# More units by rows, w_mod earlier, and group loads moved to other slots in a fused attention and gMLP kernel

## The chip, the cores and the metric

One core of one Trainium2 chip. The metric is the time of one execution in device microseconds (us).

## The reference, cut to what matters

```python
mod = (silu(c) @ w_mod).reshape(1, 6, 1, 512)         # sa, ca, ga, sb, cb, gb
h = layernorm(x) * (1 + ca) + sa
q = (h @ wq)                                           # 32 heads of 128; 8 groups of 4 heads share k, v
p = softmax(q @ k.T / sqrt(128))                       # 2048 queries x 2048 keys
x = x + ga * ((p @ v) @ wo)
h = layernorm(x) * (1 + cb) + sb
z = gelu(h @ w_in); z1, z2 = halves of z; z2 = layernorm(z2)
x = x + gb * ((z1 * (w_sp @ z2 + b_sp)) @ w_out)
```

## The kernel before

A *unit* is one query tile of 128 rows of one group of 4 heads: 8 groups x 16 tiles = 128 units. *Iteration* u is the stretch of code with the scores of unit u, in eight *slots*: in each, two score matmuls, one exp of 1024 columns on ScalarE (ACT), a part of an older unit's weighted sum, and one matmul of the q projection or the output projection. A plain unit computes its scores transposed, and its weighted sum uses p as the weights, 64 matmuls of 129 columns. A unit *by rows* computes scores row-wise, divides by the row sum on VectorE (DVE), turns each head with a DMA transpose issued from SyncE, and needs 16 matmuls of 512 columns, but two iterations later.

```python
TURN_A, TURN_B = 3 * CT, (HKV - 1) * NT                # 12, 112
def by_rows(u):
    return TURN_A <= u < TURN_B and u % 2 == 0
def pv_at(u):                                          # iteration of the weighted sum
    return u + 3 if by_rows(u) else u + 1
...
def turn_rows(u, hh):                                  # two slots after the head's second exp
    ... row sum, reciprocal, multiply on DVE ...
    nc.sync.dma_start_transpose(out=pTs[u][:, :, hh * P : (hh + 1) * P], in_=pn[hh])
...
def mod_rows():                                        # gate rows through DRAM
    ...
        nc.gpsimd.dma_start(out=line[:]..., in_=modc[:, cols])
        nc.gpsimd.dma_start(out=rows[:], in_=line[:].partition_broadcast(P))
...
at(9, 4, mod_cols_b)                                   # at(iteration, slot, work)
at(10, 4, mod_rows)
...
for g in range(1, HKV):
    it = (g - 1) * NT
    at(it + 7, 6, lambda g=g: load_k(g))               # SyncE, a transposing load
    at(it + 8, 3, lambda g=g: load_v(g))               # POOL
    at(it + 9, 3, lambda g=g: load_wo(g, nc.gpsimd))   # POOL
    at(it + 7, 3, lambda g=g: load_wq(g, nc.gpsimd))   # POOL
```

`pn[0..2]` lie in the memory of `win_sb`, `pn[3]` in that of `wmod_a`; a unit's head can be exponentiated into them only when the turn of two units before has been read out.

Of the kernel before, what the change touches and what calls it, by code (L numbers as in the profile page):

```python
# [10 lines left out]
BF16 = mybir.dt.bfloat16  # L11
# [4 lines left out]
P = 128  # L16
# [559 lines left out]
def kernel(  # L576
# [19 lines left out]
    nc = tc.nc  # L596
    _, S, D = A_x.shape
    _, HKV, SK, DH = A_k_cache.shape
# [6 lines left out]
    NT = S // P  # L605
    NDT = D // P
    NKT = SK // P
    NFT = FH // P
    NCH = S // 512
    CT = 512 // P  # L610
    FC = _f_chunk(FH)
    NFHC = FH // FC
    NSLOT = NKT // 2
# [14 lines left out]
    win_dram = B_w_in.rearrange("(dt p) f -> p dt f", p=P)  # L628
# [15 lines left out]
    late = free_b.enter_context(tc.tile_pool(name="late", bufs=2, side="right"))  # L644
# [12 lines left out]
    win_sb = win_t[:].rearrange("p (k f) -> p k f", k=NDT)  # L657
# [13 lines left out]
    def bank2():  # L671
        return psum.tile([P, 1024], FP32, name="s_ps")
# [45 lines left out]
    def load_wq(g, engine):  # L718
        wqs[g] = early.tile([P, NDT, REP * DH], BF16, name="wq_g")
        engine.dma_start(  # L720
            out=wqs[g][:], in_=wq_dram[:, :, g * REP * DH : (g + 1) * REP * DH]
        )

    def load_v(g):
        v1 = late.tile([P, NKT, DV], BF16, name="v1")
        nc.gpsimd.memset(v1[:, :, DH:DV], 1.0)
        if g > 0:
            nc.gpsimd.dma_start(out=v1[:, :, 0:DH], in_=v_dram[:, g])
        else:
            nc.sync.dma_start(out=v1[:, 0 : NKT // 2, 0:DH], in_=v_rows)  # L730
            nc.sync.dma_start(
                out=v1[:, NKT // 2 : NKT, 0:DH], in_=v_dram[:, 0, NKT // 2 : NKT]
            )
        groups[g]["v1"] = v1

    def load_wo(g, engine):
        wo_g = late.tile([P, REP, D], BF16, name="wo_g")
        engine.dma_start(out=wo_g[:], in_=wo_dram[:, g * REP : (g + 1) * REP, :])
        groups[g]["wo"] = wo_g

    def load_k(g):
        kT = early.tile([P, SK], BF16, name="kT")
        nc.sync.dma_start_transpose(out=kT[:], in_=A_k_cache[0, g])
        groups[g] = dict(kT=kT)
# [154 lines left out]
    for k in range(2):  # L899
        for dt in (2 * k, 2 * k + 1):  # L900
# [3 lines left out]
            else:  # L904
                nc.scalar.activation(
                    out=dst,
                    in_=src,
# [17 lines left out]
    for hf, copy in enumerate((nc.vector.tensor_copy, nc.scalar.copy)):  # L925
        copy(
            out=qTs[0][:, 2 * hf : 2 * hf + 2, 0:P],
            in_=q_ps[hf][:, 0 : 2 * P].rearrange("p (h q) -> p h q", h=2),
# [33 lines left out]
    NU = HKV * NT  # L962


    TURN_A, TURN_B = 3 * CT, (HKV - 1) * NT

    def by_rows(u):
        return TURN_A <= u < TURN_B and u % 2 == 0

    def pv_at(u):  # L970
        return u + 3 if by_rows(u) else u + 1

    rsums, pTs, onorms, oTs, xaccs, o_pss, h2Ts = {}, {}, {}, {}, {}, {}, {}
    later = {}

    def at(it, slot, fn):
        later.setdefault((it, slot), []).append(fn)

    def qk(u, i):
        g, j = divmod(u, NT)  # L980
        b, jj = g * NCH + j // CT, j % CT
        if i == 0:
            if TURN_A <= u <= TURN_B + 1 and u % 2 == 1:
                pTs[u] = wspp.tile([P, NT, 512], BF16, name="wsp")
            else:
                pTs[u] = late.tile([P, NKT, 512], BF16, name="pT")
            if by_rows(u):
                rsums[u] = stat.tile([P, NSLOT], FP32, name="rs")
        s_ps = bank2()
        if by_rows(u):  # L990
            hh, half = divmod(i, 2)
            for c in range(2):
                k0 = (2 * half + c) * 512
                nc.tensor.matmul(  # L994
                    s_ps[:, c * 512 : (c + 1) * 512],
                    lhsT=qTs[b][:, hh, jj * P : (jj + 1) * P],
                    rhs=groups[g]["kT"][:, k0 : k0 + 512],
                    start=True,
                    stop=True,
                )  # L1000
            nc.scalar.activation(  # L1001
                out=pn[hh][:, half * HK : (half + 1) * HK],
                in_=s_ps[:],
                func=ACT.Exp,
                scale=inv_sqrt_dh,
                accum_out=rsums[u][:, i : i + 1],
            )
            if half == 1:
                at(*divmod(u * NSLOT + i + 2, NSLOT), lambda: turn_rows(u, hh))
            return  # L1010
        for h in range(2):
            kt = 2 * i + h
            nc.tensor.matmul(  # L1013
                s_ps[:, h * 512 : (h + 1) * 512].rearrange("p (r q) -> p r q", r=REP),
                lhsT=groups[g]["kT"][:, kt * P : (kt + 1) * P],
                rhs=qTs[b][:, :, jj * P : (jj + 1) * P],
                start=True,
                stop=True,
            )
        nc.scalar.activation(  # L1020
            out=pTs[u][:, 2 * i : 2 * i + 2, :],
            in_=s_ps[:].rearrange("p (k q) -> p k q", k=2),
            func=ACT.Exp,
            scale=inv_sqrt_dh,
        )
# [150 lines left out]
    def load_wsp(tile_, t, st):  # L1176
        nc.sync.dma_start_transpose(
            out=tile_[:, st, :],
            in_=B_w_sp[t * 512 : (t + 1) * 512, st * P : (st + 1) * P],
        )  # L1180

    wsp = [None] * NCH
# [33 lines left out]
    ln1_at(2, (2, 4), (3, 1), (4, 5))  # L1216
    ln1_at(3, (5, 1), (5, 5), (7, 4))
    at(2, 5, lambda: nc.gpsimd.dma_start(out=wmod_b, in_=wmod_dram[:, :, 2 * D : NMOD]))
    at(TURN_B + 3, 5, lambda: nc.gpsimd.dma_start(out=win_sb, in_=win_dram))
    at(9, 4, mod_cols_b)  # L1220
    at(10, 4, mod_rows)

    def set_fill(b):


        hole = TURN_A + 1 if (TURN_A + 1) // CT == b - 1 else None
        fs = qproj(b, list(range(REP)), 0, 512, ("misc", "o_ps" if hole else "misc"))
        for k, fn in enumerate(fs):
            it, slot = (b - 1) * CT + k // NDT, k % NDT
            if hole:  # L1230
                it, slot = hole, k // 2
            if b == 1:
                it, slot = 2 + (10 + k) // 16, (5 + k // 2) % 8
            elif b == 2:
                it, slot = (5, k // 2) if k < 8 else (it, slot)
            fill.setdefault((it, slot), []).append(fn)
# [1 line left out]
    def wsp0():  # L1238
        wsp[0] = wspp.tile([P, NT, 512], BF16, name="wsp")

    at(TURN_B + 4, 0, wsp0)
    for st in range(NT):
        at(TURN_B + 4 + st // 2, 2 + 4 * (st % 2), lambda st=st: load_wsp(wsp[0], 0, st))
    for g in range(1, HKV):
        it = (g - 1) * NT
        at(it + 7, 6, lambda g=g: load_k(g))
        at(it + 8, 3, lambda g=g: load_v(g))
        at(it + 9, 3, lambda g=g: load_wo(g, nc.gpsimd))
        at(it + 7, 3, lambda g=g: load_wq(g, nc.gpsimd))


    zs = {}
# [90 lines left out]
    for it in range(NU + 6):  # L1343
        if it < NU:
            if it % CT == 0 and it // CT + 1 < NB:
                set_fill(it // CT + 1)
        elif it == NU:
            free_a.close()
            z2p = fast.enter_context(tc.tile_pool(name="z2p", bufs=1))
            zs["z2"] = z2p.tile([P, NT, FH], BF16, name="z2")  # L1350
        pvs = [u for u in (it - 3, it - 1) if 0 <= u < NU and pv_at(u) == it]
        wos = [u for u in (it - 5, it - 3) if 0 <= u < NU and pv_at(u) + 2 == it]
        wf = [fn for u in wos for fn in wo_proj(u)]
        for i in range(NSLOT):
            for fn in later.pop((it, i), []):
                fn()
            if it < NU:
                qk(it, i)
            if len(pvs) == 1:
                pv_part(pvs[0], i, NSLOT)  # L1360
            elif pvs:
                n = NSLOT // 2
                pv_part(pvs[i // n], i % n, n)
            for fn in fill.pop((it, i), []):
                fn()
            if i >= NSLOT - len(wf):
                wf[i - NSLOT + len(wf)]()
            if it >= NU:
                zrun(3)
        for u in wos:  # L1370
            if u >= (HKV - 1) * NT:
                ln2(it, u % NT)
        if it == NU + 2:
            free_b.close()
            mlp = fast.enter_context(tc.tile_pool(name="mlp", bufs=1, side="right"))
            zs["z1T"] = mlp.tile([P, NFT, S], BF16, name="z1T")
            wout_sb = mlp.tile([P, NFT, D], BF16, name="wout_sb")
            bsp_bc = mlp.tile([P, S], BF16, name="bsp_bc")
            nc.gpsimd.dma_start(out=wout_sb[:], in_=wout_dram)
            nc.gpsimd.dma_start(out=bsp_bc[:], in_=B_b_sp.partition_broadcast(P))  # L1380
# [11 lines left out]
    for f in range(NFT):  # L1392
# [6 lines left out]
        out=ok1[:], in0=rall[:], scalar1=1.0 / SAFE, scalar2=None, op0=ALU.is_ge  # L1399
# [8 lines left out]
        out=bad[:], in0=okm[:], scalar1=-1.0, scalar2=1.0, op0=ALU.mult, op1=ALU.add  # L1408
# [137 lines left out]
```

## Time and profile before

| | before |
|---|---|
| median of the first 3 executions | 1316.68 us (1314.65 to 1318.89) |
| span of the profiled execution | 1314.1 us |
| TensorE busy | 99% |
| ACT, DVE busy | 84%, 50% |
| turns (512 KB SBUF to SBUF), issue to landing | 4.2 / 4.6 / 13.3 us least, median, most |

Busy shares are averages, and TensorE's 99% hide short waits. How start times show them, and the lines, are in the prediction.

### The profile page before, as it was taken

To read this page: it belongs to the slowest core of one execution; us is meant where nothing else is said; L and a number is where in the kernel's file an instruction comes from. 1 tells how busy PE (TensorE), PEld (TensorE's weight loads), DVE (VectorE), ACT (ScalarE), POOL (GpSimd) and SP (SyncE) were. 2 spreads that over 40 slices of the span, in tenths; PEclk is the share of its full clock that TensorE was granted. 3 is DMA by queue.
4 is the path that set the end of the run, shared out by engine and by line. 5 is a ranking of instruction groups with operands and counts; after the bars stand their busy time and mean duration, and the time that the engine had idled before them with its cause. 6 is when DMAs were issued, how large, how long until landed. Compare 5 with 4: busy or idle time off the path is not lost.

```text
span 1314.1 us, 25092 instructions
## 1 busy us (share of the span) xinstructions
PE 1305.1 (99%) x9959; PEld 755.5 (57%) x9959; DVE 657.4 (50%) x1612; ACT 1105.0 (84%) x1461; POOL 52.0 (4%) x96
## 2 busy tenths in 40 slices
PE   9999999999999999999999999999999999999998
PEld 5666555555555555555555555555556666644445
DVE  6624445444454544444455544444452566784444
ACT  7899999999999999999999999999998899650000
POOL 1101000000000000000000000000000000120000
PEclk9999999999999999999999999999999999999999
DMA  7554988878988888988897877688762232143200
GB/s 181 123 67 58 180 161 141 140 125 158 153 144 138 144 141 138 135 142 157 153 143 129 155 141 144 124 166 151 140 126 76 45 62 48 29 117 80 69 21 27
DMA packets 537741, 156.79 MB, mean 119 GB/s; under 512 B 527280, under 2 KB 533680, under 8 KB 537616
## 3 DMA queue, kind: packets, MB, share of 16 engines
q1 hardware_dynamic: 530592, 135.97, 60.3%
q0 software_dynamic: 4432, 16.91, 4.6%
q10 hardware_dynamic: 2592, 2.23, 0.5%
q8 instruction: 80, 1.31, 0.4%
q14 instruction: 45, 0.37, 0.1%
HBM read 21.89 MB, written 2.10 MB: 18 GB/s over the span
## 4 chain that ended last, share of the span: by engine, by line
PE 98%; DMA 1%; DVE 0%; issue 0%; ACT 0%; ACTq 0%; DVEq 0%
PE o_ps L1069 21%; PE s_ps L1013 20%; PE o_ps L1048 13%; PE s_ps L994 13%; PE misc L1101 8%; PE misc L944 8%; PE misc L1426 7%; PE s_ps L1260 2%; PE s_ps L1299 2%; PE o_ps L1447 1%; DMA pT<-wmod_a 1%; PE o_ps L785 1%; PE s_ps L1447 1%; PE misc L854 0%; PE o_ps L944 0%; DVE hT L813 0%
## 5 line engine op out<-in xcount | busy, mean ns | idle before, releaser
L1020 ACT ACTIVATE wsp<-s_ps 128x1024 bf16<-128x1024 f32 x408 | 416.2, 1025 | 19.5 <-PE s_ps L1013 3.5
L1013 PE MATMUL s_ps<-qT,kT 128*128 128x512 bf16 x1248 | 370.9, 379 | 1.9 <-ACT wmod_a L1001 1.6
L1001 ACT ACTIVATE win_sb<-s_ps 128x1024 bf16<-128x1024 f32 x300 | 307.0, 1025 | 6.2 <-ACT win_sb L1001 0.8
L1069 PEld LDWEIGHTS <-wsp 128*128 128x128 bf16 x3264 | 218.5, 98 | 96.3
L1069 PE MATMUL o_ps<-v,wsp 128*128 128x129 bf16 x3264 | 251.6, 220 | 0.0
L994 PE MATMUL s_ps<-kT,qT 128*128 128x512 bf16 x800 | 237.9, 379 | 0.0
L1048 PE MATMUL o_ps<-pT,v 128*128 128x512 bf16 x800 | 237.3, 379 | 0.0
L1020 ACT ACTIVATE pT<-s_ps 128x1024 bf16<-128x1024 f32 x216 | 217.3, 1026 | 20.6 <-PE s_ps L1013 8.3
L1101 PE MATMUL misc<-wo_g,oT 128*128 128x512 bf16 x512 | 194.0, 379 | 0.0
L1013 PEld LDWEIGHTS <-kT 128*128 128x128 bf16 x1248 | 121.0, 98 | 117.0 <-issue 4.4
L944 PE MATMUL misc<-hT,wq_g 128*128 128x512 bf16 (+2 forms) x520 | 187.0, 371 | 0.1
L1069 PEld LDWEIGHTS <-pT 128*128 128x128 bf16 x1728 | 115.3, 98 | 49.6
L955 DVE CAST qT<-misc 128x512 bf16<-128x512 f32 x125 | 85.5, 684 | 112.2 <-PE misc L944 112.2
L1048 PEld LDWEIGHTS <-v 128*128 128x128 bf16 x800 | 78.2, 98 | 94.4
L1069 PE MATMUL o_ps<-v,pT 128*128 128x129 bf16 x1728 | 132.5, 220 | 0.0
L1057 DVE CAST oT<-o_ps 128x512 bf16<-128x512 f32 x50 | 34.6, 691 | 173.7 <-PE o_ps L1048 173.7
L1035 DVE TENSOR_SCALAR win_sb<-win_sb,rall 128x2048 bf16<-128x2048 bf16 x150 | 113.0, 753 | 5.7 <-DVE rall L1034 0.5
L994 PEld LDWEIGHTS <-qT 128*128 128x128 bf16 x800 | 78.2, 98 | 52.5 <-issue 0.2
L1001 ACT ACTIVATE wmod_a<-s_ps 128x1024 bf16<-128x1024 f32 x100 | 102.4, 1024 | 2.3 <-DMA pT<-wmod_a 2.3
L1426 PE MATMUL misc<-wsp,z 128*128 128x512 bf16 (+2 forms) x560 | 100.7, 336 | 0.0
L1080 DVE RECIPROCAL rall<-o_ps 128x2 f32<-128x2 f32 x156 | 26.6, 170 | 135.1 <-PE o_ps L1069 131.4
L1031 DVE TENSOR_TENSOR tot<-rs 128x1 f32<-128x1 f32 x200 | 30.7, 154 | 120.6 <-ACT win_sb L1001 119.1
(106 smaller groups left out, 856.5 us busy)
## 6 DMA issues: line engine op xcount, KB each, us to landing
wq_g<-in_A_wq_dram POOLq DMA_DIRECT2D x7, 512.0 KB, 5.5
v<-in_A_v_cache_dram POOLq DMA_DIRECT2D x7, 512.0 KB, 5.9
wo_g<-in_A_wo_dram POOLq DMA_DIRECT2D x7, 512.0 KB, 3.8
pT<-win_sb SPq DMA_TRANSPOSE x150, 4.9
wsp<-in_w_mod_dram POOLq DMA_DIRECT2D x1, 2048.0 KB, 10.4
out_dram<-yout ACTq DMA_DIRECT2D x16, 128.0 KB, 1.7
win_sb<-in_B_w_in_dram POOLq DMA_DIRECT2D x1, 1792.0 KB, 9.3
x_sb<-in_A_x_dram SPq DMA_DIRECT2D x3, 512.0 KB, 5.3
```

Of the source, the lines that this page charges most:

```text
L944: nc.tensor.matmul(ps[0][:, o0 : o0 + n], lhsT=wqs[g][:, dt, hh * DH : (hh + 1) * DH], rhs=hTs[ch][:, dt, c0 : c0 + n], start=(dt == 0), s ...
L955: nc.vector.tensor_copy(out=dst, in_=src)
L994: nc.tensor.matmul(s_ps[:, c * 512 : (c + 1) * 512], lhsT=qTs[b][:, hh, jj * P : (jj + 1) * P], rhs=groups[g]["kT"][:, k0 : k0 + 512], sta ...
L1001: nc.scalar.activation(out=pn[hh][:, half * HK : (half + 1) * HK], in_=s_ps[:], func=ACT.Exp, scale=inv_sqrt_dh, accum_out=rsums[u][:, i : ...
L1013: nc.tensor.matmul(s_ps[:, h * 512 : (h + 1) * 512].rearrange("p (r q) -> p r q", r=REP), lhsT=groups[g]["kT"][:, kt * P : (kt + 1) * P], ...
L1020: nc.scalar.activation(out=pTs[u][:, 2 * i : 2 * i + 2, :], in_=s_ps[:].rearrange("p (k q) -> p k q", k=2), func=ACT.Exp, scale=inv_sqrt_dh,)
L1035: nc.vector.tensor_scalar(out=pn[hh], in0=pn[hh], scalar1=rinv, scalar2=None, op0=ALU.mult)
L1048: nc.tensor.matmul(o_pss[u][:], lhsT=groups[g]["v1"][:, kt, 0:DH], rhs=pTs[u][:, kt, :], start=(kt == 0), stop=(kt == NKT - 1),)
L1057: nc.vector.tensor_copy(out=oTs[u][:], in_=o_pss[u][:].rearrange("p (r q) -> p r q", r=REP))
L1069: nc.tensor.matmul(o_ps[:, hh % 2, 0 : DH + 1], lhsT=pTs[u][:, kt, hh * P : (hh + 1) * P], rhs=groups[g]["v1"][:, kt, 0 : DH + 1], start=( ...
L1101: nc.tensor.matmul(X_ps[:], lhsT=oTs[u][:, hh, :], rhs=groups[g]["wo"][:, hh, :], start=(hh == 0), stop=(hh == REP - 1),)
L1426: nc.tensor.matmul(g_ps[:, :n], lhsT=z2[:, st, f * P : (f + 1) * P], rhs=wsp[t][:, st, c0 : c0 + n], start=(st == 0), stop=(st == NT - 1 a ...
```

## The change

The intent: more units with the cheaper weighted sum (even units 8 to 120 in place of 12 to 110), the homes of the tiles chosen so that the third one, where w_mod's second part sits at first, is free in time, and group loads spread out so that each pair of units has one.

```diff
-    TURN_A, TURN_B = 3 * CT, (HKV - 1) * NT
+    TURN_A, TURN_B = 2 * CT, NU - CT - 2
...
+    users, homes = dict(pT0=-2, pT1=-1, wsp=CT + 2), {}
+    for u in range(NU):
+        homes[u] = min(users, key=lambda k: users[k])
...
-    at(TURN_B + 3, 5, lambda: nc.gpsimd.dma_start(out=win_sb, in_=win_dram))
-    at(9, 4, mod_cols_b)
-    at(10, 4, mod_rows)
+    at(NU - CT - 1, 2, lambda: nc.gpsimd.dma_start(out=win_sb, in_=win_dram))
+    at(4, 4, mod_cols_b)
+    at(5, 4, mod_rows)
...
-                it, slot = hole, k // 2
+                it, slot = divmod(hole * NSLOT + k // 2 - 1, NSLOT)
...
-        at(TURN_B + 4 + st // 2, 2 + 4 * (st % 2), lambda st=st: load_wsp(wsp[0], 0, st))
+        at(NU + 1 + st // 4, 2 * (st % 4), lambda st=st: load_wsp(wsp[0], 0, st))
...
-        at(it + 7, 6, lambda g=g: load_k(g))
-        at(it + 8, 3, lambda g=g: load_v(g))
-        at(it + 9, 3, lambda g=g: load_wo(g, nc.gpsimd))
-        at(it + 7, 3, lambda g=g: load_wq(g, nc.gpsimd))
+        at(it + 7, 4, lambda g=g: load_wq(g, nc.gpsimd))
+        at(it + 9, 5, lambda g=g: load_k(g))
+        at(it + 11, 4, lambda g=g: load_v(g))
+        at(it + 13, 4, lambda g=g: load_wo(g, nc.gpsimd))
```

More of the change, by code (lines that the diff above doesn't have):

```diff
@@ L971, in pv_at @@
         return u + 3 if by_rows(u) else u + 1
+    users, homes = dict(pT0=-2, pT1=-1, wsp=CT + 2), {}
+    for u in range(NU):
+        homes[u] = min(users, key=lambda k: users[k])
+        assert users[homes[u]] < u
+        users[homes[u]] = pv_at(u)
     rsums, pTs, onorms, oTs, xaccs, o_pss, h2Ts = {}, {}, {}, {}, {}, {}, {}
@@ L982, in qk @@
         if i == 0:
-            if TURN_A <= u <= TURN_B + 1 and u % 2 == 1:
+            if homes[u] == "wsp":
                 pTs[u] = wspp.tile([P, NT, 512], BF16, name="wsp")
             else:
-                pTs[u] = late.tile([P, NKT, 512], BF16, name="pT")
+                pTs[u] = late.tile([P, NKT, 512], BF16, name=homes[u], bufs=1)
             if by_rows(u):
@@ L1239, in wsp0 @@
         wsp[0] = wspp.tile([P, NT, 512], BF16, name="wsp")
-    at(TURN_B + 4, 0, wsp0)
+    at(NU + 1, 0, wsp0)
     for st in range(NT):
-        at(TURN_B + 4 + st // 2, 2 + 4 * (st % 2), lambda st=st: load_wsp(wsp[0], 0, st))
+        at(NU + 1 + st // 4, 2 * (st % 4), lambda st=st: load_wsp(wsp[0], 0, st))
     for g in range(1, HKV):
         it = (g - 1) * NT
-        at(it + 7, 6, lambda g=g: load_k(g))
-        at(it + 8, 3, lambda g=g: load_v(g))
-        at(it + 9, 3, lambda g=g: load_wo(g, nc.gpsimd))
-        at(it + 7, 3, lambda g=g: load_wq(g, nc.gpsimd))
+        at(it + 7, 4, lambda g=g: load_wq(g, nc.gpsimd))
+        at(it + 9, 5, lambda g=g: load_k(g))
+        at(it + 11, 4, lambda g=g: load_v(g))
+        at(it + 13, 4, lambda g=g: load_wo(g, nc.gpsimd))
     zs = {}
@@ L1350 @@
             zs["z2"] = z2p.tile([P, NT, FH], BF16, name="z2")
-        pvs = [u for u in (it - 3, it - 1) if 0 <= u < NU and pv_at(u) == it]
-        wos = [u for u in (it - 5, it - 3) if 0 <= u < NU and pv_at(u) + 2 == it]
+        pvs = [u for u in (it - 5, it - 3, it - 1) if 0 <= u < NU and pv_at(u) == it]
+        wos = [u for u in (it - 7, it - 5, it - 3) if 0 <= u < NU and pv_at(u) + 2 == it]
         wf = [fn for u in wos for fn in wo_proj(u)]
```

## The prediction

> **What bounds the kernel now.** I read the page's busy times first, then who waited for whom on TensorE, then the matmuls in order of time. In what follows a unit is one query tile of one group (128 of them); it has eight slots, and a slot is two score matmuls, one exp of 1024 columns and a share of older work. Iteration u is the stretch of code that does the scores of unit u.
>
> ```profile
> span 1314.1 us, 25092 instructions
> PE 1305.1 (99%) x9959; PEld 755.5 (57%) x9959; DVE 657.4 (50%) x1612; ACT 1105.0 (84%) x1461; POOL 52.0 (4%) x96
> ...
> PE s_ps L1013 <- ACT wmod_a L1001: 1.6, 1, 1.6
> PE o_ps L785 <- DVE onorm L767: 1.2, 1, 1.2
> PE s_ps L1013 <- ACT pT L1020: 0.2, 1, 0.2
> ```
>
> The first two lines are the page, the last three all of TensorE's visible waits: 3.0 us. But a 512-column matmul is recorded as 379 ns although the next one starts after some 216 ns, so short waits hide in the overlap. I therefore went to start times. The first three lines are a slot of a plain unit (scores transposed, weighted sum by columns), the last three a slot in which a unit "by rows" has its weighted sum:
>
> ```profile
> 80.57 0.59 PE L1013 MATMUL s_ps<-qT,kT 128*128 128x512 bf16 x2
> 81.00 0.62 PE L1069 MATMUL o_ps<-v,pT 128*128 128x129 bf16 x8
> 81.45 0.38 PE L944 MATMUL misc<-hT,wq_g 128*128 128x512 bf16 x1
> ...
> 402.05 0.59 PE L1013 MATMUL s_ps<-qT,kT 128*128 128x512 bf16 x2
> 402.48 0.59 PE L1048 MATMUL o_ps<-pT,v 128*128 128x512 bf16 x2
> 402.91 0.38 PE L944 MATMUL misc<-hT,wq_g 128*128 128x512 bf16 x1
> ```
>
> The eight 129-column matmuls take 0.45 us (81.00 to 81.45), the two of 512 columns that do the same work 0.43. Counting 16 score matmuls to a unit gives the start of each iteration, and the table of stretches for some of them:
>
> ```profile
> 80.57:89.37 8.80, 8.80 (x89) 5.97 (x88) 2.38 (x7) 8.19 (x9) 0.00 (x0) 1.00 0.08 15
> 393.24:402.05 8.81, 8.81 (x90) 5.97 (x89) 5.62 (x15) 8.43 (x16) 0.00 (x0) 1.00 0.79 135
> 402.05:410.68 8.63, 8.63 (x41) 3.92 (x40) 2.86 (x8) 8.30 (x10) 0.00 (x0) 1.00 1.05 179
> 1080.67:1089.48 8.81, 8.81 (x90) 5.98 (x89) 5.86 (x16) 8.20 (x9) 0.79 (x2) 1.00 0.41 62
> 117.39:149.09 31.70, 31.70 (x238) 17.96 (x237) 16.35 (x42) 31.17 (x49) 1.76 (x2) 1.00 0.98 158
> ```
>
> After the stretch come length, then busy time of PE, weight loads, DVE, ACT, POOL. In order: a plain iteration (8.80 us); a pair of the alternation, with the weighted sum of a plain unit (8.81) and of a unit by rows (8.63); a plain one of the last group; iterations 12 to 15, where the alternation begins. In all but the last TensorE issues a matmul whenever the one before allows it: taking N/2.4 + 2.5 ns for N columns, the waits summed over all 128 iterations and the tail are 11.9 us, of which some 5 are at the start, 1.8 in iteration 60, and 1.2 in iterations 12 to 15. There ACT is the bound (31.17 of 31.70 busy). So the kernel is bound by the number of matmul columns on TensorE, nearly everywhere, and a change of the schedule alone can win back a few us at most.
>
> **What the Trainium skill says.** "TensorE: Matmul & The Clock Gate", Back-to-back issue gap, gives N/2.4 + 2.5 ns for a warm array: 215.8 ns at 512 columns, 56.3 at 129. The trace agrees (0.43 us for two, 0.45 for eight). The same section gives about 81 ns for a sustained N=128 stream with weight loads; this trace does not show that, its loads (98 ns recorded) overlap. "Perfetto Trace Analysis", Identifying the Most-Contended Engine, says that matmul busy time is no measure of how near TensorE is to its limit; iterations 12 to 15 agree, busy 31.70 of 31.70 us for 30.5 us of columns. "DMA: Bandwidth & Descriptors", Issuing engines are not separate DMA queues, says that transfers issued from different engines interleave on the same 16. The 1.8 us of iteration 60 agrees with it:
>
> ```profile
> 528.39 0.22 PE misc L944
> 528.82 13.25 DMA pT<-wmod_a
> 542.25 0.85 issue
> 543.34 0.59 PE s_ps L1013 x2
> ```
>
> This is the chain of waits. The turn of unit 58's last head was issued at 528.82, a 512 KB load of wq_g at 528.90; they landed after 13.3 and 12.2 us, where such a turn takes 4.6 in the median. The exp that writes wmod_a again came too late.
>
> **The change, part by part.** *Units by rows.* Before, the even units 12 to 110 (50 of them); after, 8 to 120 (57). Each of the 7 turns 64 matmuls of 129 columns into 16 of 512: 64 x 56.25 = 3.60 us against 16 x 215.8 = 3.45, or by the stretches 8.81 - 8.63 = 0.18 us. 7 x 0.176 = **1.23 us less**. ACT cannot give more, since it is not the bound in those iterations: its exps are the same 8 a unit, 8.2 us plain, and about as much by rows (8.3 to 8.4 in the pair, with the accumulator reads). So the gain is only in columns.
>
> *The hole.* Where the alternation begins, one iteration has no weighted sum. The hole, iteration 13 before, is 9 after. It holds the 16 q matmuls of one block in both; after, two of them go into slot 7 of iteration 8 and the last of each step sits one slot earlier. Columns in the four iterations: 30.5 us both times, ACT still the bound at about 31.7. I put 0.2 us on the better placing.
>
> *The end of the alternation.* Iteration 113 took 12.26 us before because two weighted sums fell in it, and 115 took 9.98 with 8 output projections and 4 q matmuls: 0.34 us of waits. After, these are iterations 123 and 125, and 125 has no q matmul left. Iterations 124 to 127 last 8.00 us each for 7.92 of columns, since ACT is the bound: 125 has room for the extra projections without a wait beyond its 8.78 us of columns. Some **0.4 us less**. The 3.4 us of the second weighted sum remain.
>
> *w_mod.* Iterations 9 and 10 lose 0.8 us each (9.61 against 8.81), 4 and 5 gain it. Iteration 4 was held by ACT at 8.00 for 7.92 of columns, so 0.08 us less. The load was issued at 37.1 and landed 10.4 us later, at 47.5; slot 4 of iteration 4 comes at some 49.4. It fits by 2 us.
>
> *Group loads.* The three from POOL keep their order (wq, v, wo), and nothing shows that they follow their place in the code: wq of group 3 stood in iteration 39, and was issued at 249.87 us, in iteration 27.
>
> ```profile
> 249.87 0.75 POOL L720 DMA_DIRECT2D wq_g<-in_A_wq_dram  x1 [64.68 <-PE misc L944]
> ...
> 306.58 1.16 POOL L728 DMA_DIRECT2D v<-in_A_v_cache_dram  x1 [0.26 <-issue]
> ...
> 323.94 0.76 POOL L738 DMA_DIRECT2D wo_g<-in_A_wo_dram  x1 [16.20 <-PE misc L1101]
> ```
>
> POOL runs ahead and stops only until the buffer of the group before last is free. So for groups 3 to 7 I expect the same moments as now, and the clash of wq with a turn stays possible. Only k moves, by two iterations, with 7 to spare. For group 1 they come later, after the writes of the gate rows: about 82 us in place of 59, needed from 117 on.
>
> *Buffers.* I followed the choice of homes by hand: the units by rows alternate between two tiles and the plain ones keep the third, so the slack is that of now (each free one iteration before use).
>
> *w_sp and w_in.* 16 turns of 1.26 us issue each move from iterations 116-123 to 129-132, where SP sits in waits; they push the later w_sp turns from 1160 to about 1168. The first product with them starts at 1184.9, the second tile's at 1214, which is late enough. w_in, issued in iteration 123 (some 1090 us) and landed 9.3 us later, is needed from 1130.
>
> Sum: -1.23 - 0.2 - 0.4 - 0.1 = -1.9 us. I add 0.5 for new small waits: 1316.68 - 1.4 = **1315.3 us**.
>
> **The rivals.** *A full DVE in the last group.* A plain iteration there has 5.86 us of DVE. A unit by rows adds 4 x (154 + 164 + 753) ns = 4.28 and 0.69 for its copy, and saves two normalisations of 0.59: 15.5 us in a pair of 17.4, 89%. It is in bursts (about 2.9 us at the end of each iteration), and a late copy out of PSUM would stop TensorE. Against it: every bank has four slots or more of slack. If it happens, 0.5 us in each of ten iterations: about 1320. *ACT as the bound*, so that the 1.23 us don't come: it is within 0.4 us of TensorE in the alternation, yet the 8.63 iterations show no wait. That gives 1316.5. *Clashes of transfers.* w_mod late by some us, or the group 1 loads on top of unit 8's turns: 1317 to 1320. If instead the loads do spread out and the clash of iteration 60 goes, another 1.8 us: 1313.
>
> **Range and chances.** The three times before spread over 4.2 us (1314.65 to 1318.89), more than the change's sum. From 1312, where the clash goes too, to 1319, where a rival takes 4 us: 8 in 10. Two per cent is 26 us: none of the 11.9 us of waits, nor any rival, reaches that, which leaves small chances for a real stall and next to none for a gain.
>
> **What would show it.** Right: L1048 has 912 matmuls in place of 800 and L1069 4544 in place of 4992; iterations 112 to 122 alternate 8.81 and 8.63; 8 to 15 take 66.4 us in place of 68.5, of which 1.6 is w_mod moved; wq of groups 3 to 7 is still issued in the iterations as before. Wrong: TensorE waiting for DVE (misc, o_ps) in 112 to 123, for w_mod in iteration 4, or for w_sp after 1185; or a time under 1311, which would mean that waits went which I did not see.

## The result, and the profile after

1315.53 us median of 4 runs (1314.65 to 1316.79), beside 1315.66 of the kernel before (4 runs, 1313.84 to 1318.89). The ratio is 0.9997, 95% interval 0.9974 to 1.002: the same. (Ratios are the mean time of one kernel's fast runs over that of the other's of the same rounds, so not quite the ratio of the medians quoted.) A second comparison, on chip 15, gave 1316.97 against 1315.60, ratio 1.001.

The page's first lines, and TensorE's longest waits, after:

```profile
span 1313.5 us, 24523 instructions
PE 1293.9 (99%) x9452; PEld 740.6 (56%) x9623; DVE 683.1 (52%) x1675; ACT 1109.7 (84%) x1517; POOL 53.9 (4%) x96
```

```profile
PE s_ps L1020 <- ACT wmod_a L1008: 1.3, 2, 0.8
PE o_ps L785 <- DVE onorm L767: 1.2, 1, 1.2
PE misc L1108 <- DMA oT<-onorm: 1.1, 1, 1.1
```

171 matmul records are missing from this trace (9452 of 9623), so I count and time by the weight loads, which are complete: 9959 - 7 x 48 = 9623, as seven more units by rows should give. The new lines are the first (two waits of TensorE on ACT, of which the longer, 0.8 us, stands at the end of iteration 10, where ACT had waited for a turn; before there was one such wait, of 1.6 us, in another place) and the third, a wait for the transpose of a plain unit's output.

Starts of the iterations, from the weight loads, give this account (us). By weight loads, which run ahead of their matmuls, the wait that the prediction puts into iteration 60 falls into 61 (10.41 us in place of 8.63), and so it is called from here on.

| iterations | before | after | difference | what it is |
|---|---|---|---|---|
| 0 to 3 | 34.53 | 34.52 | 0.0 | |
| 4 to 7 | 35.28 | 36.86 | +1.6 | w_mod's matmuls come here |
| 8 to 15 | 68.47 | 69.04 | +0.6 | w_mod leaves (-1.6), predicted 66.4 |
| 16 to 111 | 838.94 | 837.82 | -1.1 | 61: -1.8; 29: +0.7 |
| 112 to the last weight load | 320.32 | 319.08 | -1.2 | five units by rows; room at 125 |

The new end of the alternation did what it should. Iterations 120 to 123 of the kernel after in the table of stretches (columns as in the prediction):

```profile
1058.60:1067.40 8.80, 8.70 (x88) 5.97 (x88) 8.42 (x23) 8.69 (x16) 1.28 (x2) 1.00 0.63 128
1067.40:1076.03 8.63, 8.63 (x40) 3.91 (x40) 6.50 (x18) 8.29 (x10) 1.28 (x2) 1.00 1.08 160
...
1084.80:1097.10 12.30, 12.25 (x105) 7.54 (x104) 6.57 (x17) 8.68 (x9) 1.61 (x3) 1.00 0.54 172
```

8.80 and 8.63 alternate, DVE (the fourth number with its count) has 14.9 of 17.4 us in the pair, and no wait of TensorE stands there. The start did not do what it should. Iterations 8 to 11:

```profile
81.99:90.60 8.61, 8.51 (x85) 5.85 (x86) 5.34 (x16) 8.53 (x16) 2.69 (x4) 1.00 0.94 175
90.60:98.04 7.44, 7.44 (x35) 3.31 (x34) 4.55 (x9) 6.89 (x9) 0.35 (x1) 1.00 1.11 219
98.04:107.80 9.76, 8.59 (x83) 5.72 (x84) 4.57 (x14) 7.38 (x14) 0.40 (x1) 1.00 1.10 199
107.80:116.10 8.30, 7.52 (x33) 3.08 (x32) 2.25 (x6) 8.30 (x12) 0.00 (x0) 1.00 1.15 216
```

By the weight loads these four take 34.1 us for the prediction's 30.5 us of columns. In the third TensorE is busy 8.59 of 9.76 us and ACT 7.38: neither is the bound, both wait. What for, POOL's and SyncE's timelines tell (start, length, what):

```profile
81.32 0.55 POOL L1181 DMA_DIRECT2D gb_rows<-mod  x1 [10.19 <-DMA mod<-modc]
81.86 0.76 POOL L720 DMA_DIRECT2D wq_g<-in_A_wq_dram  x1
82.60 0.23 POOL L726 MEMSET v<- 128x128 bf16 x1
82.75 1.18 POOL L728 DMA_DIRECT2D v<-in_A_v_cache_dram  x1
83.90 0.78 POOL L738 DMA_DIRECT2D wo_g<-in_A_wo_dram  x1
```

```profile
85.97 12.32 SPq L1045 DMA_TRANSPOSE wsp<-win_sb  x3
98.45 1.58 SPq L1096 DMA_TRANSPOSE oT<-onorm  x1
100.14 3.76 SPq L1045 DMA_TRANSPOSE wsp<-wmod_a  x1
```

Group 1's three loads, which in the kernel before went out at 59 to 61 us, now stand behind the gate rows in POOL's order and go out at 82 to 84 us, just ahead of the first turns of unit 8, the first by rows. The first of these turns took 9.9 us to land. The issue of three turns took SyncE 12.3 us, and the transpose of unit 7's output, next in its queue, went out at 98.45 and landed too late for its projection in iteration 10. The turn of the fourth head was issued at 100.14 and landed 7.33 us later:

```profile
100.14 7.33 DMA wsp<-wmod_a
107.47 0.02 issue
107.49 0.04 ACTq L1008
107.53 0.05 issue
107.57 0.07 ACT wmod_a L1008
107.64 0.85 issue
```

In this chain of waits the exp of unit 10 into `wmod_a` could begin only at 107.57.

### The profile page after: what moved, and what is told of

It reads as the page before. It is cut to its first block, busy times and chain, and to the rows that moved or that the text cites. A ratio compares the mean times of both kernels' runs of the same rounds, so it can differ in the third digit from the quotient of the medians.

```text
span 1313.5 us, 24523 instructions
## 1 busy us (share of the span) xinstructions
PE 1293.9 (99%) x9452; PEld 740.6 (56%) x9623; DVE 683.1 (52%) x1675; ACT 1109.7 (84%) x1517; POOL 53.9 (4%) x96
## 4 chain that ended last, share of the span: by engine, by line
PE 97%; DMA 1%; issue 1%; DVE 0%; ACT 0%; ACTq 0%; DVEq 0%
PE o_ps L1076 20%; PE s_ps L1020 19%; PE s_ps L1001 15%; PE o_ps L1055 15%; PE misc L1108 8%; PE misc L944 8%; PE misc L1433 7%; PE s_ps L1267 2%; PE s_ps L1306 2%; PE o_ps L1454 1%; DMA wsp<-wmod_a 1%; PE s_ps L1454 0%; DMA wmod_a<-in_w_mod_dram 0%; PE misc L854 0%; PE o_ps L785 0%
## 5 line engine op out<-in xcount | busy, mean ns | idle before, releaser
L1027 ACT ACTIVATE pT<-s_ps 128x1024 bf16<-128x1024 f32 x560 | 567.9, 1025 | 33.1 <-PE s_ps L1020 10.4
L1076 PEld LDWEIGHTS <-pT 128*128 128x128 bf16 x4480 | 299.5, 98 | 130.8
L1008 ACT ACTIVATE win_sb<-s_ps 128x1024 bf16<-128x1024 f32 x342 | 349.9, 1024 | 7.4 <-PE s_ps L1001 1.1
L1076 PE MATMUL o_ps<-v,pT 128*128 128x129 bf16 x4480 | 344.9, 220 | 1.2
L1020 PE MATMUL s_ps<-qT,kT 128*128 128x512 bf16 x1136 | 337.8, 379 | 2.9 <-ACT wmod_a L1008 1.3
L1055 PE MATMUL o_ps<-wsp,v 128*128 128x512 bf16 x442 | 132.7, 379 | 0.6
L1055 PE MATMUL o_ps<-pT,v 128*128 128x512 bf16 x426 | 128.6, 379 | 0.6
L1433 PEld LDWEIGHTS <-z 128*128 128x128 bf16 x560 | 50.6, 98 | 48.5
L1121 DVE TENSOR_TENSOR xacc<-misc,xacc 128x512 f32<-128x512 f32 x112 | 76.2, 680 | 0.0
L944 PEld LDWEIGHTS <-wq_g 128*128 128x128 bf16 x528 | 50.4, 98 | 29.3 <-issue 0.4
```

Source lines behind the costliest of these rows:

```text
L944: nc.tensor.matmul(ps[0][:, o0 : o0 + n], lhsT=wqs[g][:, dt, hh * DH : (hh + 1) * DH], rhs=hTs[ch][:, dt, c0 : c0 + n], start=(dt == 0), s ...
L1008: nc.scalar.activation(out=pn[hh][:, half * HK : (half + 1) * HK], in_=s_ps[:], func=ACT.Exp, scale=inv_sqrt_dh, accum_out=rsums[u][:, i : ...
L1020: nc.tensor.matmul(s_ps[:, h * 512 : (h + 1) * 512].rearrange("p (r q) -> p r q", r=REP), lhsT=groups[g]["kT"][:, kt * P : (kt + 1) * P], ...
L1027: nc.scalar.activation(out=pTs[u][:, 2 * i : 2 * i + 2, :], in_=s_ps[:].rearrange("p (k q) -> p k q", k=2), func=ACT.Exp, scale=inv_sqrt_dh,)
L1055: nc.tensor.matmul(o_pss[u][:], lhsT=groups[g]["v1"][:, kt, 0:DH], rhs=pTs[u][:, kt, :], start=(kt == 0), stop=(kt == NKT - 1),)
L1076: nc.tensor.matmul(o_ps[:, hh % 2, 0 : DH + 1], lhsT=pTs[u][:, kt, hh * P : (hh + 1) * P], rhs=groups[g]["v1"][:, kt, 0 : DH + 1], start=( ...
```

## The experiments

TensorE's columns had saved what was expected at the end of the alternation, so the theory was: **columns plus clash**. The change saves the predicted 1.9 us of columns and small waits, and the loads on top of the turns take it back. The rivals: the placing of the q matmuls in the hole, the new slots of the loads, or that units by rows save nothing.

All ran correctly. The edits are shown shortened, with several lines put on one. Chip and kernel before alongside are in the table; 8 to 11 is the length of those iterations in the profiled execution, and the spread is the highest minus the lowest run.

| run | chip | median us (spread, runs) | before alongside | ratio, interval | 8 to 11 |
|---|---|---|---|---|---|
| c_g1_early | 9 | 1316.18 (5.1, 4) | 1314.22 | 1.001, 0.999 to 1.003 | 34.15 |
| d_old_slots | 9 | 1317.40 (3.1, 4) | 1314.22 | 1.0019, 1.0003 to 1.0036 | 36.33 |
| g_old_hole | 9 | 1315.82 (1.1, 4) | 1314.22 | 1.0011, 0.9994 to 1.0028 | 34.35 |
| e_sp_loads | 9 | 1312.37 (0.9, 4) | 1314.22 | 0.9984, 0.9968 to 1.0001 | 31.80 |
| h_before_sp | 9 | 1313.97 (1.5, 6) | 1314.17 | 0.9996, 0.9982 to 1.001 | 37.31 (plain, with w_mod) |
| i_late_rows | 9 | 1312.41 (0.4, 5) | 1314.17 | 0.9983, 0.9968 to 0.9998 | 31.80 |
| f_columns | 9 | 1321.05 (0.7, 4) | 1314.17 | 1.005, 1.0033 to 1.0067 | 35.23 (plain) |
| a_start12 | 9 | 1314.84 (3.4, 4) | 1314.17 | 1.0003, 0.9986 to 1.002 | 35.23 (plain) |
| j_wq_pool | 9 | 1312.99 (1.2, 4) | 1316.29 | 0.997, 0.995 to 0.999 | 31.80 |
| k_g1_pool | 9 | 1314.35 (0.9, 4) | 1316.29 | 0.998, 0.996 to 1.000 | 33.64 |
| l_after_again | 15 | 1316.97 (4.9, 6) | 1315.60 | 1.001, 0.9993 to 1.0027 | 36.06 |
| m_sp_again | 15 | 1312.48 (0.3, 6) | 1315.60 | 0.9974, 0.996 to 0.9988 | 31.80 |

The kernel before had a median of 1314.2 and of 1316.3 us on the same chip 9. So a difference of 1 us to a median of it means little, and the lengths of iterations carry the argument.

**c_g1_early: group 1's loads ahead of the gate rows.**

```diff
+    at(5, 2, lambda: load_wq(1, nc.gpsimd)); at(5, 2, lambda: load_v(1)); at(5, 2, lambda: load_wo(1, nc.gpsimd))
     at(5, 4, mod_rows)
...
-        (the three loads of group 1 in iterations 7, 11, 13)
```

> The changed kernel with one edit: POOL issues group 1's three loads (wq, v, wo) before the writes of the gate rows, so at about 58 us as in the kernel before, not at 82 to 84. Theory (clash): iterations 8 to 11 lost 2.4 us (34.1 us for 30.5 of columns) because these loads landed on the first turns of unit 8. Then they take about 31.7 us here, the first turn of unit 8 lands in 4 to 6 us and not 9.9, and the time is some 2.4 us under that of the changed kernel (about 1313). Rival (hole): the q matmuls of the new hole, or ACT, made the loss; then iterations 8 to 11 stay at 34 us and the time at 1315.5.

A miss. The loads did go out at 60 to 62 us, but 8 to 11 stayed at 34.15 us, the first turn of unit 8 took 11.1 us, and iteration 7 grew by 1.4 us. POOL's timeline of this run shows why the edit was no clean test:

```profile
78.56 0.56 POOL L1181 DMA_DIRECT2D ga_rows<-mod  x1 [14.71 <-DMA mod<-modc]
79.11 0.76 POOL L1180 DMA_DIRECT2D mod<-modc  x1
87.91 0.55 POOL L1181 DMA_DIRECT2D gb_rows<-mod  x1 [8.04 <-DMA mod<-modc]
99.29 0.75 POOL L720 DMA_DIRECT2D wq_g<-in_A_wq_dram  x1 [10.83 <-PE o_ps L944]
```

The gate rows slid to where the loads had been, and gb_rows went out at 87.91 beside the turn of 87.56. The rival of the hole is not proved by this; the theory had to be wider: whatever POOL sends there may hold up the turns.

**d_old_slots: the loads in their old slots.**

```diff
-        at(it + 7, 4, load_wq) ; at(it + 9, 5, load_k) ; at(it + 11, 4, load_v) ; at(it + 13, 4, load_wo)
+        at(it + 7, 6, load_k) ; at(it + 8, 3, load_v) ; at(it + 9, 3, load_wo) ; at(it + 7, 3, load_wq)
```

> The changed kernel with the group loads in the slots that they had before (k in iteration 7, v in 8, wo in 9, wq in 7 of each group). Theory: POOL issues in its own order as buffers come free, so wq, v and wo of groups 3 to 7 are issued in the same iterations as in both kernels (wq in 27, 43, ... slot 3 or 4), group 1's still follow the gate rows at 82 us, and iterations 8 to 11 keep 33.5 to 34.5 us; time 1315.5 within 1.5. Rival (slots): the new places of the loads cost the time; then 8 to 11 fall to about 31.7 and the time to 1313.

POOL's loads kept their moments: group 1's at 83.8 to 85.9 us, and the later wq as in the changed kernel (254.34 here, 251.80 there, both in iteration 27). So the part of the change that spreads the loads moved only k. The sum of 8 to 11 was longer than expected, 36.3 us (TensorE waited 3.0 us for one transpose of an output), and the time 1317.4, outside the stated 1.5. k now goes out at 76.2 us, before unit 8's turns; whether that made it worse, or the clash only fell out worse in this execution, one profile can't say (the changed kernel itself showed 34.1 and, in its second profile, 36.1).

**g_old_hole: the q matmuls of the hole as before.**

```diff
-                it, slot = divmod(hole * NSLOT + k // 2 - 1, NSLOT)
+                it, slot = hole, k // 2
```

> The changed kernel with the old placing of the q matmuls in the hole (two in each slot of iteration 9, none in slot 7 of 8). Theory: the loss of 8 to 11 is the transfers', so it stays, 33.5 to 34.5 us, and the time is 1315.5 within 1.5. Rival (hole): the shift of one slot made the loss; then 8 to 11 take about 31.7 us and the time is 1313.

As the theory has it: 34.35 us and 1315.82. The hole is not the cause.

**e_sp_loads: all group loads from SyncE, in its free slots.**

```diff
-        at(it + 7, 4, lambda g=g: load_wq(g, nc.gpsimd))
+        at(it + 7, 5, lambda g=g: load_wq(g, nc.sync))
         at(it + 9, 5, lambda g=g: load_k(g))
-        at(it + 11, 4, lambda g=g: load_v(g))             # its copy from POOL
-        at(it + 13, 4, lambda g=g: load_wo(g, nc.gpsimd))
+        at(it + 11, 5, lambda g=g: load_v(g))             # its copy from SyncE
+        at(it + 13, 5, lambda g=g: load_wo(g, nc.sync))
```

> The changed kernel with all group loads issued from SyncE, in order with the turns, in slot 5 of iterations 7, 9, 11 and 13 of each group, where SyncE has no turn to issue: one load per pair of units in fact and not only in the code. Theory: no load falls on a turn any more, so no turn takes over 9 us, iterations 8 to 11 take about 31.7 us, and the single waits of the kind of iteration 61 before (1.8 us) or 29 after (0.7 us) are gone; time 3 us under the changed kernel, about 1312.5. Rival: a plain load in SyncE's queue holds up the turns behind it; then turns land later than 4.6 us in the median and the time is 1316 or more.

1312.37 us, and 31.80 us for the four iterations, 0.1 from what was expected. The same stretches as above, and TensorE's waits, all of them:

```profile
82.10:90.70 8.60, 8.60 (x87) 5.85 (x86) 5.33 (x16) 8.52 (x16) 0.77 (x2) 1.00 0.99 139
90.70:98.20 7.50, 7.50 (x36) 3.31 (x35) 4.62 (x9) 6.91 (x10) 0.00 (x0) 1.00 0.99 195
98.20:106.70 8.50, 8.49 (x86) 5.75 (x85) 4.54 (x14) 8.50 (x16) 0.00 (x0) 1.00 1.02 160
106.70:113.90 7.20, 7.20 (x33) 3.05 (x32) 2.13 (x6) 7.20 (x10) 0.00 (x0) 1.00 1.07 192
```

```profile
PE o_ps L785 <- DVE onorm L767: 1.2, 1, 1.2
PE misc L854 <- DMA wmod_a<-in_w_mod_dram: 0.4, 2, 0.2
PE s_ps L1020 <- ACT pT L1027: 0.2, 1, 0.2
```

ACT is busy all through the third and fourth, so it is the bound again, as in iterations 12 to 15 of the kernel before. SyncE issues the same transposes in 8.34 us in place of 12.32, and unit 7's output goes out at 94.59 in place of 98.45:

```profile
86.08 8.34 SPq L1045 DMA_TRANSPOSE wsp<-win_sb  x3
94.59 1.44 SPq L1096 DMA_TRANSPOSE oT<-onorm  x1
96.12 1.73 SPq L1045 DMA_TRANSPOSE wsp<-wmod_a  x1
```

Iterations 16 to 111 take 837.12 us, without a wait. The longest turn took 6.2 us.

One part of the expectation was wrong: loads still fall on turns. Of the 21 loads of wq, v and wo, 20 went out while a turn was under way, 1.4 to 2.1 us after the issue of that turn, and those turns took 4.3 to 4.7 us. In the changed kernel the wq loads of POOL from 251.80 on went out 0.2 to 0.7 us after the issue of a turn, and those turns took 6.3 to 12.3 us. The edit changes two things at once: this moment, and the DMA queue (the page lists q1, hardware_dynamic, for SyncE's transfers and q0, software_dynamic, for POOL's). No run separates them, so which of the two spares the turns is not shown; that the moment matters among POOL's own loads, the traces show (table below).

**h_before_sp: the kernel before with the same loads from SyncE.** The edit is that of e_sp_loads, on the kernel before.

> The kernel before with one edit: group loads from SyncE in slot 5 of iterations 7, 9, 11 and 13 of each group. It tells what of the 1312.4 us of e_sp_loads comes from the loads and what from the units by rows. Theory (columns): e_sp_loads differs from this one by the sum of the prediction alone, 1.9 us, so this one comes out at about 1314.2 us, with no wait of 1.8 us in iteration 61, and the stretches of e_sp_loads are the shorter by 0.18 us in each odd iteration from 113 to 121 and by 0.3 to 0.6 at 123 to 125. Rival (loads): the units by rows give nothing and the loads everything; then this one is at 1312.4 too, and the sum of the iterations is the same.

1313.97 us, only 0.2 below the kernel before, so the loads from SyncE are worth little there in the median. In the profiled execution iteration 61 took 8.63 us in place of 10.41. From iteration 0 to the last weight load this run took 1296.2 us and e_sp_loads 1294.3: 1.8 us, where the prediction's sum had 1.9. But 0.5 us of this is a wait that the edit itself brought into iteration 11 of h_before_sp (9.29 us; 8.81 in the kernel before). Without it the change itself is worth 1.4 us: 0.2 in iterations 4 to 15 (103.58 in e_sp_loads, 103.75 in the kernel before) and 1.2 from 112 on. The medians, i_late_rows below against this run, differ by 1.6.

**i_late_rows: e_sp_loads with the gate rows sent in iterations 17 to 21 from SyncE.**

```diff
-            nc.gpsimd.dma_start(out=line..., in_=modc[:, cols]); nc.gpsimd.dma_start(out=rows[:], in_=line...)
+            at(17, 5, nc.sync.dma_start(out=line..., in_=modc[:, cols]))
+            at(19 + 2 * i, 5, nc.sync.dma_start(out=rows[:], in_=line...))
```

> e_sp_loads with the gate rows' writes and reads through DRAM moved off POOL's early stretch (60 to 90 us) to SyncE's quiet slots in iterations 17, 19 and 21. Theory: in e_sp_loads the gate rows still overlap unit 8's first turn (83 to 90 us) but no wait of TensorE came of it, so iterations 8 to 11 stay at 31.8 us and the time at 1312.4 within 0.7. Rival: the gate rows hold the first turns up as the loads did; then 8 to 11 fall by another 0.5 us or more.

31.80 us again, 1312.41. In e_sp_loads the gate rows cost no time that could be measured.

**f_columns: no unit by rows.**

```diff
-        return TURN_A <= u < TURN_B and u % 2 == 0
+        return False
-        hole = TURN_A + 1 if (TURN_A + 1) // CT == b - 1 else None
+        hole = None
```

> The changed kernel with no unit by rows at all (and no hole). It sizes the whole saving by columns: 57 units at 0.176 us are 10.0 us more on TensorE; against that the iterations with too few columns for ACT, 8 to 11, go (34.1 - 30.5 = 3.6 us less), and the clash of iteration 29 (0.7). Theory: 1315.5 + 10.0 - 3.6 - 0.7 = 1321 us, every iteration from 16 to 123 at 8.81. Rival: units by rows are worth nothing by columns and only shift waits; then the time is 1312 or less.

1321.05 us where 1321 was worked out, every iteration from 16 to 123 at 8.81. It sizes the saving (57 units at 0.176 us), and it is a control for the spread: without turns the runs lie within 0.7 us.

**a_start12: the early start undone.**

```diff
-    TURN_A, TURN_B = 2 * CT, NU - CT - 2
+    TURN_A, TURN_B = 3 * CT, NU - CT - 2
```

> The changed kernel with the units by rows starting at 12 again (the early start undone; w_mod early, the new end and the loads kept). Theory (clash): the two early units save 0.35 us by columns and cost 2.4 us by the clash with group 1's loads and the gate rows, so without them iterations 8 to 15 take about 67.0 us in place of 69.0 and the time falls by some 2 us, to 1313.5, although fewer units go by rows. Rival: the early start paid as predicted; then this is 0.4 us slower than the changed kernel.

Iterations 8 to 15 took 67.03 us, as expected, 2.0 less than in the changed kernel: two units fewer by rows, and faster there. The time, 1314.84, was 1.3 us above what was expected. In the profiled execution iteration 61 had a wait again (9.89 us): a turn issued at 529.17 took 12.7 us beside the wq load of 529.26.

**j_wq_pool and k_g1_pool: e_sp_loads with one thing given back each,** wq of groups 2 to 7 to POOL, or group 1's three loads to POOL.

```diff
+        at(it + 7, 4, lambda g=g: load_wq(g, nc.sync if g < 2 else nc.gpsimd))     # j_wq_pool
+        ... nc.gpsimd if g == 1 else nc.sync, for wq, v and wo                     # k_g1_pool
```

> e_sp_loads with one thing given back: wq of groups 2 to 7 is issued by POOL again, as soon as the buffer is free (slot 3 or 4 of iterations 11, 27, 43, ..., when the last head of a unit by rows is turned). Theory (clash of wq): the turns of that moment are slow again in some executions, at least one above 6.5 us and in some above 11, one or two of iterations 29, 45, 61, ... are longer by up to 1.8 us, and the runs spread by 1 us or more where those of e_sp_loads lay within 0.9; median 1312.5 to 1314.5. Rival: v and wo were the cause; then nothing comes back, and it is 1312.4 within 0.5.

> e_sp_loads with the other thing given back: group 1's wq, v and wo are issued by POOL, behind the gate rows, at 82 to 84 us; all later groups stay with SyncE. Theory (clash at the start): the first turn of unit 8 takes 9 us or more, TensorE waits for the turn of unit 7's output in iteration 10, and iterations 8 to 11 take 33 to 35 us in place of 31.8, nothing else changes; time 1312.4 + 1.5 to 2.5. Rival: it was wq of group 2 at 98 us that held up iterations 10 and 11; then 8 to 11 stay at 31.8 here.

k_g1_pool is as the theory has it: the first turn took 9.9 us, 8 to 11 went from 31.80 to 33.64, and the time from 1312.37 to 1314.35 (same chip; j_wq_pool had 1312.99). Only the wait named was another: not the transpose of the output but the exp into `wmod_a`.

```profile
PE s_ps L1020 <- ACT wmod_a L1008: 1.5, 1, 1.5
PE o_ps L785 <- DVE onorm L767: 1.2, 1, 1.2
PE s_ps L1020 <- ACT pT L1027: 0.2, 1, 0.2
```

j_wq_pool is half shown. Turns beside wq were slow again (249.86 us: 9.6 us, and four more of 6.9 to 7.3), but none so late that TensorE waited in the profiled execution; the runs spread by 1.2 us against 0.9, which is not a clear difference.

**l_after_again and m_sp_again: both once more, on one chip with the kernel before.** No edit.

> The changed kernel once more, beside the kernel before and e_sp_loads on one chip, for the spread and for a comparison in the same rounds. Theory: its columns save 1.9 us and the clash at the start costs about 2.4, so it is within 1 us of the kernel before; its runs spread by 2 us or more, as those of the kernel before do. Rival: the first comparison hid a gain; then it is 2 us faster than the kernel before.

> e_sp_loads once more, on the same chip as the changed kernel. Theory: faster than the changed kernel by 2.4 us (start) to 4 us (with other clashes), runs within 1 us of each other. Rival: its 1312.4 came from the chip; then it lies within 1 us of the changed kernel.

The changed kernel 1316.97 (1314.54 to 1319.46), e_sp_loads 1312.48 (1312.39 to 1312.72). The spread of 4.9 us against 0.3 is a sign that the clashes are what differs between executions; only one execution of each set was profiled, so it is not shown for the others. The longest turns of the kernel before, the changed one and e_sp_loads show it in the profiles too (their turn's line, time from issue to landing):

```profile
DMA to landing us min/median/max: 4.2/4.6/13.3
```

```profile
DMA to landing us min/median/max: 4.2/4.4/12.3
```

```profile
DMA to landing us min/median/max: 4.2/4.5/6.2
```

The traces of all runs together say more about the moment. In the 14 profiled executions 41 wq loads of POOL went out within 0.9 us of the issue of a turn:

| the load's issue, from the turn's | turns | the turn's time to landing, us |
|---|---|---|
| 0.16 to 0.80 us earlier | 7 | 5.6 to 6.1, one 7.3 |
| 0.05 us later | 1 | 8.8 |
| 0.08 to 0.22 us later | 6 | 9.6 to 13.3 |
| 0.25 to 0.30 us later | 4 | 6.8 to 8.5 |
| 0.39 to 0.67 us later | 23 | 6.1 to 7.9 |

The four slowest are 13.25, 12.74, 12.28 and 11.64 us (kernel before, a_start12, changed kernel, d_old_slots), and the iterations in which their buffer was needed were longer by 1.8, 1.3, 0.7 and 0.1 us (61, 61, 29 and 45). So some 0.1 us of issue time lies between such a wait and none (at 0.21 and 0.22 us later no wait followed). This is a comparison across runs and not an experiment; why the load has this effect is not shown. Group 1's three loads are another case: they went out 0.6 to 4.9 us ahead of the first turn, which then took 9.9 to 12.0 us.

So e_sp_loads beats both kernels: by 1.9 to 3.1 us in the medians of the rounds it shared with the kernel before, and by 4.5 us on chip 15 over the changed one. It is still within 2% of all of them.

## Why the prediction was right or wrong

The time was within the range. Step by step:

- **The bound** was right. TensorE's columns are the bound outside of a few stretches; f_columns came out at 1321.05 for 1321 worked out from 0.176 us a unit and the stretches measured before.
- **Units by rows, -1.23 us:** right in the size, from the measured 8.81 - 8.63 (its other working, 3.60 - 3.45, would give 0.15 a unit and not 0.18). The odd iterations 113 to 121 are 0.17 to 0.18 us shorter than a plain one, apart from 113 and 115, which also lose the double work. For the two early units, 8 to 15 take 66.73 us in e_sp_loads against 67.03 in a_start12.
- **The end, -0.4:** right. 113 and 123 together lose 0.18 us, which is the saving of one unit; 115 and 125 lose 0.54, of which 0.17 is a unit.
- **The hole, -0.2:** wrong. With the loads out of the way 8 to 11 took 31.80 us, against 31.64 for 12 to 15 before: the new placing costs some 0.2 us and gains none. So the sum of -1.9 was too large, and -1.4 came.
- **w_mod** was right: 1.6 us moved, and no wait in iteration 4 of this kernel. The load was nearer to late than the 2 us worked out: in g_old_hole and k_g1_pool a weight load waited 0.2 us for it there.
- **Group loads:** the moments were right, for group 1 (82 us) and for the later ones (iteration 27 and so on). The conclusion was wrong. I asked when the loads are needed, found 117 us, and put no cost into the sum for the transfers beside which they go out; that was left to a rival. Unit 8's turns went out at 86 to 100 us, the first 2.1 us after the last of the three loads.
- **"I add 0.5 for new small waits"** is the term of the sum that failed. Iterations 8 to 11 alone lost 2.3 us in the profiled execution (34.11 against 31.80 without the clash) and 4.3 in the second one, and iteration 29 another 0.7 in the first. One of the rivals had it ("the group 1 loads on top of unit 8's turns: 1317 to 1320"), and the changed kernel's runs reach up to 1319.5.
- **The DVE rival** was rightly put aside: the pair of units 120 and 121 had 14.9 us of DVE work in 17.4 (I had worked out 15.5), and TensorE never waited for DVE there.

That 1315.53 lies so near to 1315.3 is luck. The forecast was 1.4 us less than 1316.68, a base of three runs; with the fourth the median before is 1315.66, and the difference that was measured is 0.1. And this 0.1 hides a larger miss: in the profiled execution the new waits took 3.0 us (2.3 and 0.7), while the wait of iteration 61 (1.8 us) did not occur, though the loads had not spread out as the hopeful rival asked: there the load followed the turn by 0.50 us and not by 0.08. It came back in a_start12.

So the change moved the time by nothing, not because its idea was worth nothing: some 1.4 us came, and the change's own new neighbourhood of transfers took 2.3 us or more. What stays open: whether SyncE's loads spare the turns by their moment alone or also by their queue; and which single transfer is too much. Group 1's three loads alone are enough (k_g1_pool). In c_g1_early the gate rows and group 2's wq were there in their stead and cost as much, and I did not separate those two. Whether a turn beside a wq load takes 13 us or 6 goes with the gap between the two issues (table above), but why is not shown.

## What to carry to other kernels

For a load that an engine issues far ahead of its place in the code, find its moment in the trace (what frees its buffer, what stands before it in that engine's order), and then ask what other transfers it meets there, not only when its data are needed. Where transfers on the critical path must not be held up, issuing the others from the same queue in known slots gives control of the moment. In the changed kernel this was worth more (4.5 us on chip 15) than the change itself (1.4), and it took the spread of the runs from 5 us to under 1; in the kernel before the medians of one call differ by 0.2 us. When a kernel is bound by one engine's columns, add up the columns first: they fix the gain, here 0.18 us a unit.

## What the Trainium skill lacked or had wrong

- "TensorE: Matmul & The Clock Gate", Back-to-back issue gap: its 81 ns for a sustained stream of N=128 matmuls with weight loads is not what this kernel shows. The section's formula, which it keeps for an isolated matmul, fits instead: eight matmuls of 129 columns, each with its own weight load, took 0.45 us, 56 ns each, through whole iterations.
- "DMA: Bandwidth & Descriptors", Issuing engines are not separate DMA queues, says that issuing from several engines only saves sequencer time. Here the issuing engine also changed the moment and the queue, and with them the time: with the loads from SyncE e_sp_loads took 1312.48 us (spread 0.3), with the loads from POOL the changed kernel took 1316.97 (spread 4.9), on the same chip.
- The same page says that transfers interleave, but gives no size for a DMA transpose beside plain loads. Here a turn takes 4.5 us in the median and 6.2 at most with the loads from SyncE (e_sp_loads; 8.4 at most in h_before_sp). A turn with a 512 KB load of POOL (wq) issued within 0.9 us of it took 5.6 to 13.3 us, most when the load came 0.08 to 0.22 us later, and the load slows too: 4.6 us for the wq load of 389.38 in the kernel before, 12.2 for that of 528.90.
